# Split weights of a Strassen-Winograd mixture kernel: made in the tiles that TensorE reads, during the first of three chunks

## The chip, the cores and the metric

One core of a Trainium2 chip runs the whole program. The metric is the device time of one execution in microseconds (us). Engine names: PE is TensorE, DVE VectorE, ACT ScalarE, POOL GpSimd, SP SyncE, whose queue (SPq) issues nearly all DMAs.

## The reference, cut to what matters

```python
scores = (q @ k.T) / 8 + bias          # 4 batches, 8 heads, 768 rows, 64 wide; 8 global columns and 96 local ones are kept
x = softmax(scores) @ v                # laid out as 3072 rows x 512
p = domain_probs / (domain_probs.sum(-1, keepdims=True) + 1e-09)
out = 0
for e in range(4):                     # w1[e]: 512 x 1024, w2[e]: 1024 x 512
    h = max(x @ w1[e], 0)
    out += p[:, e:e+1] * (h @ w2[e])
```

## The kernel before, in words

**Stage A, attention.** `attention` (line 338) is a generator of 48 two-tile steps `d`, run by the loop at line 792. Each step turns scores into a 128x256 piece of x. The rows of x fall into three chunks of 1024. The pieces of chunk 0 stay in SBUF (the tiles `x0`, named b11 to b22, trace name `b`); those of chunks 1 and 2 go to DRAM (`xt` to `xd`). Beside the steps the loop runs other generators: `mixture` (288, the normalised p, from step 26), `spread_shares` (731, p transposed and stored in DRAM, from step 30), `first_forms` (672, from step 26) and `advance` (617), which prepares weights.

**Products.** All four matrices of a product are cut 2x2, and a Strassen-Winograd scheme with seven products takes the place of eight: the weight side needs A11, A12, A22 and the sums S1 to S4, the other side B11, B21, B22 and T1 to T4. Each operand is split in two parts, `hi` (a cast to fp32r) and `lo` (the rest, subtracted), and each product is hi·hi + lo·hi + hi·lo: six matmuls of 128x512 for one product of the first layer (`product`, 650, PSUM `pm`) and six for one half of a product of the second (`half`, 902, PSUM `pq`). The casts are on ACT, the subtractions on DVE or POOL.

**Chunks.** For each chunk there are 16 first-layer items `ci` (256 hidden units each) and 8 second-layer items `cj` (512 hidden units). The loop at line 982 counts slots `s`; 14 slots make a block `j` of two `ci`, and slot `r` of a block runs one first-layer product (`small`, 840, kk = 0 to 6) and one half product of the block before (`half`). So 24 blocks and a tail of halves. `form` (833) splits a sum of h into tiles `f1` to `f5` (trace name `f`). At kk = 6 of the second `ci`, T2 of h is written to the tile X (trace name `hX`) and T3 in place of B22 (`hB`); T2 is split at r = 1 of the next block on DVE, T3 at r = 3 with its `lo` on POOL, and T4 at r = 0, on DVE in chunk 0 and on POOL later. At kk = 4 of the next block, DVE writes the new B22. In the last block of a chunk `load_x`, `sum_x` and `next_form` (699 to 726) prepare x of the next chunk.

**Weights.** `prepare` (528) loads 256 rows or columns of w1 or w2 (`raw`), makes four sums on POOL, casts and subtracts in four groups into the tile `split` (pool `outp`, two buffers), and `store` (576) writes each group to DRAM (`kept`; trace names `w`, `w_A`, `w_S`). A `split` tile takes its buffer two groups after its predecessor, and the store of that predecessor is issued just before. There are 32 such preparations in 192 steps: 58 steps in stage A (line 788; there the casts are on POOL) and the rest in chunk 0 (`pace`, line 981; casts on ACT). TensorE never reads `split`: `ask_w1` (627) and `ask_w2` (639) load the parts back from DRAM into `w1s` (six buffers) and `w2s` (four buffers), in all three chunks.

**Order.** SP and POOL keep the program's order (`Kept`, line 48) all through, and so do the casts of weights. In stage A all engines do. In the chunks DVE, ACT and PE are ordered by the framework's scheduler, by dependencies and its own estimates.

Of the kernel before, what the change touches and what calls it, by code (L numbers as in the profile page):

```python
# [18 lines left out]
P = 128  # L19
# [181 lines left out]
def attn_moe_kernel(ctx: ExitStack, tc, q, k, v, n_global, n_local, domain_probs, w1, w2, out):  # L201
# [9 lines left out]
    W1BUFS = 6  # L211
# [314 lines left out]
    GROUPS = (("A11", "A12"), ("S1", "S2"), ("S3", "S4"), ("A22",))  # L526

    def prepare(kind, i, cast):

        e, g = divmod(i, NPR)  # L530
        raw = rawp.tile([P, 2, HALF], F32, name="raw")
        if kind == 1:
            flat = raw.rearrange("p n (a f) -> p (n a) f", f=2 * P)
            sy.dma_start(flat, w1[e, :, g * 2 * P : (g + 1) * 2 * P].rearrange("(a p) f -> p a f", p=P))
            four = raw.rearrange("p n (a m f) -> p n m a f", a=2, m=2)
            a11, a21, a12, a22 = (four[:, n, m] for n in range(2) for m in range(2))
            firsts = four[:, :, 0]
        else:
            sy.dma_start(raw, w2[e, g * 2 * P : (g + 1) * 2 * P, :].rearrange("(f p) m -> p f m", p=P))
            a11, a21, a12, a22 = (raw[:, n, m * 2 * P : (m + 1) * 2 * P] for n in range(2) for m in range(2))  # L540
            firsts = raw[:, :, : 2 * P]
        yield
        sums = rawp.tile([P, 2, HALF], F32, name="raw")
        quarters = [sums[:, n, m * 2 * P : (m + 1) * 2 * P] for n in range(2) for m in range(2)]
        if kind == 1:
            s1, s2, s3, s4 = (t.rearrange("p (a f) -> p a f", a=2) for t in quarters)
        else:
            s1, s2, s3, s4 = quarters
        po.tensor_add(s1, a21, a22)
        po.tensor_sub(s2, s1, a11)  # L550
        yield
        po.tensor_sub(s3, a11, a21)
        po.tensor_sub(s4, a12, s2)
        yield
        pairs = [t.rearrange("p (n c) -> p n c", n=2) for t in (sums[:, 0], sums[:, 1])]
        for n, names in enumerate(GROUPS):
            while len(stores) > 1:
                store()
            made = outp.tile([P, 2, 2, 2 * P], F32R, name="split")
            hi, lo = (made[:, : len(names), m] for m in range(2))  # L560
            if n == 0:
                src = firsts
            elif n == 3:
                hi, lo, src = hi[:, 0], lo[:, 0], a22
            else:
                src = pairs[n - 1]
            if kind == 1 and n in (0, 3):
                hi, lo = (t.rearrange("p n (a f) -> p n a f" if n == 0 else "p (a f) -> p a f", a=2) for t in (hi, lo))
            cast(hi, src)
            po.tensor_tensor(lo, src, f32(hi), op=ALU.subtract)  # L570
            stores.append((kind, i, n, made))
            yield

    stores = []

    def store():
        kind, i, n, made = stores.pop(0)
        if kind == 1:
            some = slice(0, len(GROUPS[n]))
            to = kept[(1, i, n)] = dp.tile([P, len(GROUPS[n]), 2, 2 * P], F32R, name=f"w1_{i}_{n}")  # L580
            sy.dma_start(f32(to), f32(made[:, some]))
            return
        j, u = divmod(i, 2)
        for at, name in enumerate(GROUPS[n]):
            if (2, j, name) not in kept:
                kept[(2, j, name)] = dp.tile([P, 2, 2, 2 * P], F32R, name=f"w2_{j}_{name}")
            sy.dma_start(f32(kept[(2, j, name)][:, u]), f32(made[:, at]))

    items = [(1, 0), (1, 1), (1, 2), (2, 0), (2, 1), (1, 3)]
    for i in range(2, per, 2):  # L590
        items += [(1, i + 2), (2, i), (2, i + 1), (1, i + 3)]
    items = [it for it in items if it[1] < per]
    going = {"now": None, "next": None, "done": 0.0, "cast": nc.gpsimd.tensor_copy}

    def cast(out, src):
        tc.keep_in_program_order(going["cast"](out, src))  # L596

    def step_weights():

        if going["now"] is None and items:  # L600
            going["now"] = prepare(*items.pop(0), cast)
            next(going["now"])
            going["at"] = 0
        if going["now"] is None:
            while stores:
                store()
            return False
        if going["at"] == 2 and items:
            going["next"] = prepare(*items.pop(0), cast)
            next(going["next"])  # L610
        next(going["now"], None)
        going["at"] += 1
        if going["at"] == 6:
            going["now"], going["next"], going["at"] = going["next"], None, 0
        return True

    def advance(steps):
        going["done"] += steps
        while going["done"] >= 1.0:
            going["done"] -= 1.0  # L620
            step_weights()
# [3 lines left out]
    ORDER2 = (("A11", "B11"), ("A12", "B21"), ("S1", "T1"), ("S2", "T2"), ("S4", "B22"), ("S3", "T3"), ("A22", "T4"))  # L625

    def ask_w1():
# [7 lines left out]
        sy.dma_start(f32(t[:, : len(names)]), f32(kept[(1, ci % per, n)]))  # L635
# [3 lines left out]
    def ask_w2():  # L639
# [7 lines left out]
        sy.dma_start(f32(t), f32(kept[(2, cj % NJ, name)]))  # L647
        w2t[(cj, name)] = t

# [22 lines left out]
    def first_forms(T1):  # L672

        b11, b12, b21, b22 = (x0[n] for n in BLOCKS)
        for k in range(2):
            def form(name, src):
                x_form(name, src, po, (k,), k == 0)
            form("B11", b11)
            po.tensor_sub(T1[:, k], b12[:, k], b11[:, k])
            yield  # L680
            form("B21", b21)
            yield
            form("T1", T1)
            po.tensor_sub(b12[:, k], b22[:, k], b12[:, k])
            yield
            form("T3", b12)
            po.tensor_add(b11[:, k], b12[:, k], b11[:, k])
            yield
            form("T2", b11)
            po.tensor_sub(b21[:, k], b21[:, k], b11[:, k])  # L690
            yield
            form("T4", b21)
            yield
            form("B22", b22)
            yield
# [3 lines left out]
    def load_x(c):  # L699
# [355 lines left out]
```

## Time and profile before

| | us |
|---|---|
| median of 2 runs | 1401.97 (1399.25 to 1404.68) |
| the profiled execution | 1399.54 |
| its span, first to last instruction | 1397.7 |
| PE busy (matmul) | 1198.4, 86% of the span |
| DVE / POOL / ACT busy | 852.4 / 567.9 / 493.7 |

The span is shorter than the time of the execution by what lies before the first and after the last instruction, 1.8 us. A line of the timeline has start, duration, engine, line, operation, out<-in, shape and count (instructions of one kind may be merged), and in brackets the idle time of the engine before it and what ended it. L42 and L57 are the wrappers through which all engines are called, so tiles tell the places.

### The profile page before, as it was taken

How to read it: one execution, taken by the hardware profiler on the slowest of the kernel's cores; microseconds unless marked ns; L12 is line 12 of the kernel's file. 1: busy time of each engine (PE TensorE's matmuls, PEld its weight loads, DVE VectorE, ACT ScalarE, POOL GpSimd, SP SyncE). 2: the span in 40 equal slices, each digit the busy share in tenths (PEclk: the TensorE clock that was granted, in tenths of full speed). 3: DMA queues.
4: the chain of work that ended last, by engine and by line, in shares of the span. 5: the costliest groups of instructions: out<-in, count | busy, mean ns of one | idle time of the engine just before them, and what ended most of it. 6: DMA issues, size and time to landing. Idle time of an engine off the chain costs nothing.

```text
span 1397.7 us, 17631 instructions
## 1 busy us (share of the span) xinstructions
PE 1198.4 (86%) x6177; PEld 940.9 (67%) x6177; DVE 852.4 (61%) x1416; ACT 493.7 (35%) x1010; POOL 567.9 (41%) x449
## 2 busy tenths in 40 slices
PE   9996896876776667778599999999889999999996
PEld 7885675654554555556478777787668877777774
DVE  6885673534453454537964677766776656776763
ACT  6775672423222232223324222222334322222222
POOL 4546864556554554665622222222532122222221
PEclk9998998999988788889899999999999999999999
DMA  9998897777776767587567565665648655565623
GB/s 216 247 260 226 236 289 241 258 247 252 258 255 226 248 226 260 208 301 274 183 199 229 182 189 159 201 203 182 224 125 257 205 174 179 183 185 175 196 91 108
DMA packets 218623, 299.14 MB, mean 214 GB/s; under 512 B 113984, under 2 KB 144800, under 8 KB 218528
## 3 DMA queue, kind: packets, MB, share of 16 engines
q1 hardware_dynamic: 216784, 297.55, 66.7%
q8 instruction: 51, 0.84, 0.2%
q10 hardware_dynamic: 1744, 0.39, 0.1%
q14 instruction: 44, 0.36, 0.1%
HBM read 228.64 MB, written 69.26 MB: 213 GB/s over the span
## 4 chain that ended last, share of the span: by engine, by line
PE 41%; DVE 18%; POOL 12%; DMA 12%; issue 10%; ACT 4%; SPq 2%; POOLq 0%; ACTq 0%; DVEq 0%
PE pm L42 18%; PE pq L42 17%; DVE hB L42 7%; DMA w_S<-split 5%; POOL split L57 5%; DVE f L42 4%; DMA w<-split 4%; POOL f L57 4%; PE ps L42 4%; DVE sumC L42 3%; ACT f L42 2%; SPq L57 2%; PE pt L42 2%; DVE hX L42 2%; DVE pm L42 1%
## 5 line engine op out<-in xcount | busy, mean ns | idle before, releaser
L42 PE MATMUL pq<-f,w2s 128*128 128x512 f32 x2016 | 554.1, 411 | 130.9 <-DVE sumC L42 38.8
L42 PEld LDWEIGHTS pq<-f,w2s 128*128 128x128 f32 x2016 | 387.7, 196 | 250.7 <-DVE sumC L42 57.8
L57 POOL TENSOR_TENSOR f<-hB,f 128x1024 fp32r<-128x1024 f32 x89 | 215.5, 2421 | 515.3 <-ACT f L42 515.3
L42 DVE TENSOR_TENSOR sumC<-pq,sumC 128x512 f32<-128x512 f32 (+1 forms) x209 | 198.0, 948 | 207.7 <-PE pq L42 207.3
L42 PE MATMUL pm<-xT,w1s 128*128 128x512 f32 x1152 | 304.1, 397 | 7.8 <-ACT u L42 7.5
L42 PE MATMUL pm<-xB,w1s 128*128 128x512 f32 x864 | 240.2, 410 | 29.9 <-DVE hB L42 29.9
L42 PEld LDWEIGHTS pm<-xT,w1s 128*128 128x128 f32 x1152 | 217.6, 191 | 60.5 <-ACT u L42 14.7
L42 ACT CAST f<-hB 128x1024 fp32r<-128x1024 f32 x144 | 150.8, 1050 | 298.2 <-DVE hB L42 227.6
L57 POOL TENSOR_TENSOR split<-raw,split 128x512 fp32r<-128x512 f32 (+1 forms) x128 | 156.6, 1228 | 185.4 <-ACT split L596 179.9
L42 PEld LDWEIGHTS pm<-xB,w1s 128*128 128x128 f32 x864 | 169.3, 198 | 74.3 <-DVE hB L42 38.4
L42 ACT COPY u<-pm 128x512 f32<-128x512 f32 x96 | 56.2, 585 | 187.3 <-PE pm L42 156.8
L57 POOL TENSOR_TENSOR raw<-raw 128x256 f32<-128x256 f32 (+1 forms) x130 | 107.2, 843 | 16.2 <-DMA raw<-in_moe_w_dram 13.5
L42 DVE TENSOR_TENSOR hB<-pm,u 128x512 f32<-128x512 f32 x48 | 33.2, 691 | 131.2 <-POOL f L57 92.0
L42 DVE SCALAR_TENSOR_TENSOR hB<-pm,share 128x512 f32<-128x512 f32 x144 | 98.9, 687 | 14.3 <-DMA share<-shares 10.0
L42 DVE TENSOR_TENSOR f<-hB,f 128x1024 fp32r<-128x1024 f32 x55 | 87.9, 1599 | 25.0 <-ACT f L42 25.0
L42 ACT ACTIVATE pb<-pb,nmax 128x256 f32<-128x256 f32 (+1 forms) x192 | 91.8, 482 | 9.9 <-DVE nmax L42 9.9
L42 ACT COPY p<-pm 128x512 f32<-128x512 f32 x48 | 28.2, 587 | 173.0 <-PE pm L42 166.1
L596 ACT CAST split<-raw 128x256 fp32r<-128x256 f32 (+1 forms) x89 | 49.1, 564 | 105.4 <-DMA w<-split 54.5
L42 DVE TENSOR_TENSOR hB<-hB,hB 128x1024 f32<-128x1024 f32 x48 | 63.1, 1314 | 30.8 <-POOL f L57 29.9
L42 DVE COPY pT<-pt 128x512 f32<-128x512 f32 (+1 forms) x96 | 59.2, 643 | 33.4 <-PE pt L42 28.9
L42 DVE CUSTOM_DVE_ANT_0 pb<-pm,nbias 128x256 f32<-128x256 f32 (+1 forms) x192 | 64.5, 391 | 2.0 <-PE pm L42 1.9
L42 PE MATMUL pm<-early_k,early_q 64*128 64x256 f32 (+1 forms) x384 | 52.8, 394 | 7.0 <-ACT early_k L42 6.7
(107 smaller groups left out, 958.9 us busy)
## 6 DMA issues: line engine op xcount, KB each, us to landing
w1s<-w SPq DMA_DIRECT2D x144, 512.0 KB, 4.7
w2s<-w_S SPq DMA_DIRECT2D x96, 512.0 KB, 4.4
w2s<-w_A SPq DMA_DIRECT2D x72, 512.0 KB, 4.0
w<-split SPq DMA_DIRECT2D x48, 512.0 KB, 3.7
raw<-in_moe_w_dram SPq DMA_DIRECT2D x32, 512.0 KB, 4.4
w_S<-split SPq DMA_DIRECT2D x64, 256.0 KB, 4.2
w_A<-split SPq DMA_DIRECT2D x48, 256.0 KB, 2.9
w1s<-w SPq DMA_DIRECT2D x48, 256.0 KB, 3.4
```

What stands on the lines that cost most here:

```text
L42: ins = fn(*args, **kwargs)
L57: return self.tc.keep_in_program_order(fn(*args, **kwargs))
L596: tc.keep_in_program_order(going["cast"](out, src))
```

## The change

What it does: (1) In stage A six w1 items and two w2 items (`EARLY`) are prepared, now a w2 item at a time (512 rows), in buffers of `w1p`, and each is stored when two or three later groups have been made. (2) The ten other w1 items and six other w2 items are made in chunk 0 by `ask_w1` and `ask_w2` themselves: the cast (ACT) and the subtraction (POOL) write the `w1s` or `w2s` tile that TensorE reads, and the tile is stored from there to DRAM for chunks 1 and 2 (`keep_fresh`). (3) The sums of weights are made in place in the raw tile. (4) The groups of w1 are cut otherwise, `w1s` has five buffers in place of six, and asks are issued one slot later in the program (`soon`/`due`). (5) T3 of h goes to X and T2 in place of B22. (6) `first_forms` makes sums a step or more before their cast and subtractions a step behind; `mixture` waits three steps more before DVE's reciprocal, and `spread_shares` starts at step 35. (7) x of the next chunk is loaded and split in another order (`border`). The pools `rawp` (3) and `outp` (2) become `raw1p` (2) and `raw2p` (4).

```diff
-    W1BUFS = 6
+    W1BUFS = 5
...
         po.tensor_scalar(total, total, 1e-9, None, op0=ALU.add)
         yield
+        yield
+        yield
+        yield
         tc.keep_in_program_order(ve.reciprocal(psumm, psumm))
...
-    GROUPS = (("A11", "A12"), ("S1", "S2"), ("S3", "S4"), ("A22",))
+    GROUPS = (("A11", "A12"), ("S1", "A22"), ("S2",), ("S3", "S4"))
+    EARLY = ((1, 0), (1, 1), (1, 2), (2, 0), (1, 5), (2, 7), (1, 9), (1, 13))
...
+    def make(kind, i, n, to, cast):
+        if kind == 1:
+            four = raws[(1, i)].rearrange("p n (a m f) -> p n m a f", a=2, m=2)
+            a11, a21, a12, a22 = (four[:, r, m] for r in range(2) for m in range(2))
+            if n == 1:
+                po.tensor_sub(a11, a11, a21)
+                po.tensor_add(a21, a21, a22)
+            elif n == 2:
+                po.tensor_sub(a21, a22, a11)
+            elif n == 3:
+                po.tensor_sub(a12, a12, a21)
...
+        cast(hi, src)
+        po.tensor_tensor(lo, src, f32(hi), op=ALU.subtract)
+    def keep(kind, i, n, made):
+        some = len(GROUPS[n]) if kind == 1 else 2
+        to = kept[(kind, i, n)] = dp.tile([P, some, 2, 2 * P], F32R, name=f"w{kind}_{i}_{n}")
+        sy.dma_start(f32(to), f32(made[:, :some]))
+    def prepare_early():
...
+            for n in range(4 if kind == 1 else 7):
+                if len(stores) > 2:
+                    keep(*stores.pop(0))
+                t = w1p.tile([P, 2, 2, 2 * P], F32R, name="w1s")
+                make(kind, i, n, t, po.tensor_copy)
+                stores.append((kind, i, n, t))
+                yield
...
     def ask_w1():
         t = w1p.tile([P, 2, 2, 2 * P], F32R, name="w1s")
-        sy.dma_start(f32(t[:, : len(names)]), f32(kept[(1, ci % per, n)]))
+        if ci >= per or (1, ci) in EARLY:
+            sy.dma_start(f32(t[:, : len(names)]), f32(kept[(1, ci % per, n)]))
+        else:
+            make(1, ci, n, t, ac.copy)
+            fresh[(1, ci, n)] = t
+            if n == 3:
+                load_late(1)
...
     def ask_w2():
...
+        else:
+            make(2, cj, n, t, ac.copy)
+            fresh[(2, cj, n)] = t
+            if n == 6:
+                load_late(2)
...
+    def keep_fresh(kind, i, n):
+        if (kind, i, n) in fresh:
+            keep(kind, i, n, fresh.pop((kind, i, n)))
...
+    def border(c, r):
+        if r == 2:
+            load("b11", "b12")
+        elif r == 5:
+            nextx["T1"] = raw1p.tile([P, 2, HALF], F32, name="raw1")
+            po.tensor_sub(nextx["T1"], nextx["b12"], nextx["b11"])
+        elif r == 7:
+            load("b21", "b22")
+            x_form("B11", nextx["b11"], po)
+        elif r == 9:
+            x_form("T1", nextx["T1"], ve)
...
-                b11, b12, b21, b22, t2 = (hb[n] for n in ("B11", "B12", "B21", "B22", "X"))
-                ve.tensor_sub(b22, b22, b12)
+                b11, b12, b21, b22, t3 = (hb[n] for n in ("B11", "B12", "B21", "B22", "X"))
+                ve.tensor_sub(t3, b22, b12)
                 ve.tensor_sub(b12, b12, b11)
                 form("T1", b12, ve)
-                ve.tensor_add(t2, b22, b11)
-                ve.tensor_sub(b21, b21, t2)
+                ve.tensor_add(b22, t3, b11)
+                ve.tensor_sub(b21, b21, b22)
...
             small(ci, kk)
-            if kk in (1, 3):
-                ask_w1()
-            if kk == 6:
-                ask_w1()
-                ask_w1()
-            if c == 0:
-                advance(pace * (0.5 if j == 0 else 1.0))
+            soon += [(ask_w1,)] * {1: 1, 5: 2, 6: 1}.get(kk, 0)
+            if kk in (0, 2, 3, 4):
+                soon.append((keep_fresh, 1, ci, (0, 2, 3, 4).index(kk)))
         if cj > 0:
             half(cj - 1, r // 2, r % 2)
+            if r % 2 == 0:
+                soon.append((keep_fresh, 2, cj - 1, r // 2))
+            else:
+                soon.append((ask_w2,))
             if r == 0:
                 form("T4", hb["B21"], ve if c == 0 else po)
             elif r == 1:
-                form("T2", hb["X"], ve)
+                form("T2", hb["B22"], ve)
             elif r == 3:
-                form("T3", hb["B22"], po)
+                form("T3", hb["X"], po)
+        for fn, *args in due:
+            fn(*args)
+        if c + 1 < CH and j == NJ - 1:
+            border(c + 1, r)
```

## Rows read from the trace of the kernel before

**Rows 1.** Busy time by stretch: span, PE, PEld, DVE, ACT, POOL, clock, DMA share, GB/s
```profile
279.00:690.00 411.00, 295.27 (x1087) 221.40 (x1088) 208.21 (x206) 116.18 (x171) 233.85 (x186) 0.86 0.70 246
731.00:985.00 254.00, 244.06 (x1061) 195.60 (x1059) 171.22 (x184) 74.24 (x91) 57.96 (x25) 1.00 0.62 196
```

**Rows 2.** Timeline of DVE: the sum written to X, once near each block's end
```profile
264.99 1.21 DVE L42 TENSOR_TENSOR hX<-hB,hB 128x1024 f32<-128x1024 f32 x1
...
637.80 2.32 DVE L42 TENSOR_TENSOR hX<-hB,hB 128x1024 f32<-128x1024 f32 x1
690.60 1.22 DVE L42 TENSOR_TENSOR hX<-hB,hB 128x1024 f32<-128x1024 f32 x1
...
979.67 1.22 DVE L42 TENSOR_TENSOR hX<-hB,hB 128x1024 f32<-128x1024 f32 x1
1032.04 1.22 DVE L42 TENSOR_TENSOR hX<-hB,hB 128x1024 f32<-128x1024 f32 x1
...
1361.90 1.22 DVE L42 TENSOR_TENSOR hX<-hB,hB 128x1024 f32<-128x1024 f32 x1
```

**Rows 3.** Waits, 279 to 690 us: who waited for whom, total us, times, longest
```profile
POOL split L57 <- ACT split L596: 155.4, 57, 7.1
...
DVE hB L42 <- POOL f L57: 66.6, 12, 11.1
...
ACT split L596 <- DMA w<-split: 39.5, 14, 6.2
...
PE pq L42 <- DMA w2s<-w_S: 28.1, 11, 8.8
```

**Rows 4.** Waits of SP's own queue in the same stretch
```profile
SPq L57 <- POOL split L57: 244.4, 59, 9.7
```

**Rows 5.** Timeline of stage A: the last piece of x of some steps, and one reciprocal
```profile
19.44 0.42 DVE L42 TENSOR_TENSOR b<-ps,rT 128x256 f32<-128x256 f32 x1
...
113.97 0.42 DVE L42 TENSOR_TENSOR xt<-ps,rT 128x256 f32<-128x256 f32 x1
...
128.86 0.30 DVE L42 RECIPROCAL psumm<-psumm 128x24 f32<-128x24 f32 x1 [12.54 <-POOL psumm L57]
...
130.75 0.42 DVE L42 TENSOR_TENSOR xt<-ps,rT 128x256 f32<-128x256 f32 x1
...
217.69 0.42 DVE L42 TENSOR_TENSOR xt<-ps,rT 128x256 f32<-128x256 f32 x1 [3.66 <-DMA b<-xt]
```

**Rows 6.** Timeline at the seam of stage A and chunk 0
```profile
226.57 0.32 SPq L57 DMA_DIRECT2D w<-split  x1
...
229.19 0.52 SPq L57 DMA_DIRECT2D share<-shares  x1
...
238.39 0.69 DVE L42 SCALAR_TENSOR_TENSOR hB<-pm,share 128x512 f32<-128x512 f32 x1 [10.04 <-DMA share<-shares]
```

**Rows 7.** Timeline at the start of a block of chunk 1
```profile
909.47 2.40 POOL L57 TENSOR_TENSOR f<-hB,f 128x1024 fp32r<-128x1024 f32 x1 [4.67 <-ACT f L42]
...
911.91 0.69 DVE L42 TENSOR_TENSOR hB<-pm,u 128x512 f32<-128x512 f32 x1 [2.99 <-POOL f L57]
...
912.65 1.23 PEld L42 LDWEIGHTS pm<-xB,w1s 128*128 128x128 f32 x6 [0.61 <-DVE hB L42]
```

**Rows 8.** Groups by shape, whole span: busy us, mean ns of one, idle before
```profile
L57 POOL TENSOR_TENSOR split<-raw,split 128x512 fp32r<-128x512 f32 x96 | 132.2, 1382 | 141.6 <-ACT split L596 139.1
...
L57 POOL TENSOR_TENSOR raw<-raw 128x256 f32<-128x256 f32 x128 | 102.1, 817 | 16.0 <-DMA raw<-in_moe_w_dram 13.5
...
L57 POOL TENSOR_TENSOR b<-b,b 128x512 f32<-128x512 f32 x6 | 7.7, 1276 | 0.0
```

**Rows 9.** Writers of and readers from X: ns min/median/max, first and last start
```profile
L42 DVE TENSOR_TENSOR f<-hX,f x24: 1208/2440/3042, 269.6 to 1365.9; 128x1024 fp32r<-128x1024 f32 x24
```

**Rows 10.** DMA issues: KB each, median us from issue to landing
```profile
w1s<-w SPq DMA_DIRECT2D x144, 512.0 KB, 4.7
...
w<-split SPq DMA_DIRECT2D x48, 512.0 KB, 3.7
```

More of the change, by code (lines that the diff above doesn't have):

```diff
@@ L524, in attn_moe_kernel @@
     x0, xb, kept = {}, {}, {}
[L526 to L531 removed]
+    GROUPS = (("A11", "A12"), ("S1", "A22"), ("S2",), ("S3", "S4"))
+    ORDER2 = (("A11", "B11"), ("A12", "B21"), ("S1", "T1"), ("S2", "T2"), ("S4", "B22"), ("S3", "T3"), ("A22", "T4"))
+    EARLY = ((1, 0), (1, 1), (1, 2), (2, 0), (1, 5), (2, 7), (1, 9), (1, 13))
+    raws = {}
@@ L542, in prepare @@
-        yield
[L543 to L571, printed above, removed]
-            yield
@@ L574, in attn_moe_kernel @@
[L574 to L621, printed above, removed]
+            raws[(1, i)] = raw
+            return
+        e, g = divmod(2 * i, NPR)
+        rows = w2[e, g * 2 * P : (g + 2) * 2 * P, :].rearrange("(u f p) m -> f p u m", u=2, p=P)
+        raws[(2, i)] = [raw2p.tile([P, 2, HALF], F32, name="raw2") for _ in range(2)]
+        for f in range(2):
+            sy.dma_start(raws[(2, i)][f], rows[f])
@@ L623, in attn_moe_kernel, with load_late @@
+    LATE = {
+        1: [(1, i) for i in range(per) if (1, i) not in EARLY],
+        2: [(2, j) for j in range(NJ) if (2, j) not in EARLY],
+    }
+    def load_late(kind):
+        if LATE[kind]:
+            load_raw(*LATE[kind].pop(0))
     w1t, w2t = {}, {}
     asked = {1: 0, 2: 0}
-    ORDER2 = (("A11", "B11"), ("A12", "B21"), ("S1", "T1"), ("S2", "T2"), ("S4", "B22"), ("S3", "T3"), ("A22", "T4"))
+    fresh = {}
     def ask_w1():
@@ new lines, in first_forms @@
+        src = {"B11": b11, "B21": b21, "B22": b22, "T1": T1, "T2": b11, "T3": b12, "T4": b21}
+        for name, add in (
+            ("B11", "T1"), ("B21", "T3"), ("T1", "T2"), ("T3", None), ("B22", "T4"), (None, None), ("T2", None), ("T4", None),
+        ):
+            for k in range(2):
+                while lows:
+                    lo, of, hi = lows.pop()
+                    po.tensor_tensor(lo, of, hi, op=ALU.subtract)
+                if add:
+                    sums(add, k)
+                if name:
+                    form(name, src[name], k)
+                yield
@@ new lines, in first_forms, with load @@
+        while lows:
+            lo, of, hi = lows.pop()
+            po.tensor_tensor(lo, of, hi, op=ALU.subtract)
+        yield
+    nextx = {}
+    def border(c, r):
+        def load(*names):
+            for n in names:
+                nextx[n] = raw2p.tile([P, 2, HALF], F32, name="raw2")
+                sy.dma_start(nextx[n], xd[(c, n)])
+        if r == 2:
[8 more added lines that the diff above has]
+            x_form("T1", nextx["T1"], ve)
+        elif r == 10:
+            x_form("B21", nextx["b21"], po)
+            ve.tensor_sub(nextx["b12"], nextx["b22"], nextx["b12"])
+        elif r == 11:
+            x_form("T3", nextx["b12"], po)
+            ve.tensor_add(nextx["b11"], nextx["b12"], nextx["b11"])
+        elif r == 12:
+            x_form("T2", nextx["b11"], ve)
+            ve.tensor_sub(nextx["b21"], nextx["b21"], nextx["b11"])
+        elif r == 13:
+            x_form("T4", nextx["b21"], ve)
+            x_form("B22", nextx["b22"], po)
@@ L805, in attn_moe_kernel @@
                 others.remove(o)
-        if d >= 4:
-            advance(DONE_IN_A / (STEPS - 3))
-        if d in (STEPS - 8, STEPS - 7, STEPS - 6, STEPS - 5, STEPS - 4, STEPS - 3)[: W1BUFS]:
+        if d >= 4 and early_w:
+            for _ in range(2 if d % 4 == 0 else 1):
+                next(early_w, None)
+        if d == STEPS - 5:
+            for _ in early_w:
+                pass
+            for kind in (1, 2, 1, 2):
+                load_late(kind)
+        if STEPS - 5 < d <= STEPS:
             ask_w1()
```

125 lines of the change are left out of this document (52 added, 73 removed).

## The prediction

> **What bounds the kernel now.** I read the busy time by stretch first, to see whether the three chunks cost the same; then the timeline of DVE, to get the length of single blocks; then the waits of the slow stretch, of the engines and of SP's queue; then stage A and its seam.
>
> A block ends near DVE's sum into X, so the distance between two such sums is one block's length. In chunk 0 the six blocks from 264.99 to 637.80 us take 372.8 us, 62.1 each; the eight of chunk 2 from 1032.04 to 1361.90 take 329.9, 41.2 each [rows 2]. Both have the same products; chunk 0 prepares weights beside them. The blocks in which the next x is made are alike, 52.8 us (637.80 to 690.60) and 52.4 (979.67 to 1032.04) [rows 2]. So about six times 21 us lie in chunk 0, and nearly none of that is TensorE's need: between 279 and 690 us PE is busy 295 of 411 us at a mean granted clock of 0.86, in chunk 1 244 of 254 at 1.00, the level of 2.4 GHz [rows 1].
>
> No engine is full in the slow stretch. POOL, the busiest helper, works 234 of 411 us [rows 1] and waits 155 us for ACT's casts of weights; those wait among others 39.5 us in 14 waits for stores of `w` from `split` to land; DVE waits 67 us for POOL's `f` parts, which stand behind the weights in POOL's order; PE waits 28 us for weights coming back [rows 3]. SP's queue waits 244 us for POOL's `split` before a store may go [rows 4], and behind such a store stand the loads of weights that PE needs. That is a ring: store, cast, subtraction, store, with two buffers, and PE's weights hang on it.
>
> Stage A starts regular: 25 steps from 19.44 to 113.97 us, 3.78 us each. At that pace the 46th step after the first would come at 193.3; it comes at 217.69, 24.4 us late [rows 5]. One gap alone, 113.97 to 130.75, loses 13.0 us: DVE stands at the reciprocal of the mixture for 12.54 us, and POOL, whose sum it wants, is behind in weights. At the seam the share of p is issued at 229.19, behind a store at 226.57, and DVE waits 10.04 us until 238.39 [rows 6].
>
> **The change, part by part.** The sum is made against the profiled execution, 1399.5 us (span 1397.7 and 1.8 around it), 2.5 us under the median of 1402.0.
>
> *Blocks of chunk 0.* Ten of 16 w1 items and six of 8 w2 items are now made in place; their loads back from DRAM go, the stores stay. What POOL must do in a block in which everything is fresh: two w1 items of four sums at 0.82 us, three subtractions at 1.38 and one of half size at about 0.7, 8.1 us each; one w2 item of four 512-wide sums at 1.28 and seven subtractions at 1.38, 14.8; three `f` parts at 2.40. Together 38 us [rows 7, 8]. Over chunk 0 it is 10 times 8.1, 6 times 14.8 and 8 times 7.2, 227 us: POOL fits a block of 41.2 us, barely in the full ones. The ring of stores is cut: a store reads a tile that was made some slots before, so SP need not wait for POOL at it, and PE's weights need no second trip. What is late next is ACT. A cast waits until PE has left the buffer and its store has landed, and behind it on ACT stand the copies p1, u2, u3 of the products (PE waits for u2 and u3 within a slot) and the casts of h; behind POOL's subtraction stand the `f` parts; SP waits for POOL only at the raw loads, after the last group of an item. The new length: 41.2, plus T4 on DVE in place of POOL (1.21 to 2.44 us for such an operation [rows 9], I take 1.8), plus DVE's other seven two-input operations of 1024, each some 0.4 longer when POOL is busy, half of them ahead of something PE waits for (1.4), plus casts in the way of copies, which no row shows: bounded by nothing (PE's own order hides it) and by the 155 us of POOL's waits over 6.6 blocks, 23 us each [rows 3]; I take 1.6, because the subtractions are due four slots or more after the ask. That is 46 us, 16 less than 62.1, and six blocks give 97. The lower end is 41.2 (125), the upper 56 (37): eight DVE operations at the longest of rows 9, 3.04 in place of 1.21 us.
>
> Here the Trainium skill speaks against the change. The trace has one and the same DVE operation at 1.21, 2.44 and 3.04 us [rows 9]. "SBUF — State Buffer", section "Who interferes with whom", says that a DVE instruction with two SBUF inputs contends with a GpSimd instruction that reads SBUF, and that the later one blocks until the first is done. By that, a POOL that is busy nine tenths of a block meets nearly every such DVE operation; it would put the block near the upper end, the time near 1331. I keep 46, since DVE's 1024-wide operations in chunk 0, with POOL busy 57% [rows 1], are not yet that slow.
>
> *Stage A.* Making and storing stay about as many (work of ten old items against 58 steps of six to an item). A buffer is now reused five groups later and its store goes two groups before that, so POOL seldom waits for a store; DVE's reciprocal comes three steps, 11 us, later than POOL's sum; casts of x no longer wait for a sum made in the same step. I take back the 13.0 and 4 of the other 11.4: 17 (8, if POOL stays as late; 24 at most) [rows 5].
>
> *The seam.* With no store waiting in SP's queue the share can go some 7 us earlier, after four loads of weights; but new raw loads (six of 512 KB) stand before it on the DMA engines. I take 6 of 10.0 (0 to 10) [rows 6]. In the first block, whose weights are all early, I take 4.
>
> *T2 and T3.* In chunks 1 and 2 DVE's new B22 waits 2.99 us for POOL's part of T3, whose source it overwrites; PE's weight load then waits 0.61 [rows 7]. With T3 in X this wait goes. T2's chain on DVE before it stays. I count 0.4 for 13 undisturbed blocks: 5 (0 to 8).
>
> *The rest.* One `w1s` buffer less and asks a slot later: the shortest lead, of S2, is still over four slots, 12 us, against a landing of 4.7 [rows 10]; nothing, with PE's next products as cover; if it were late, 1 us in each of 48 items. `border`: one more operation on DVE, loads split in pairs; 0, and 5 either way.
>
> Sum: 97 + 17 + 6 + 4 + 5 = 129; 1399.5 − 129 = **1270 us**.
>
> **The rivals.** *DVE and POOL in each other's way.* POOL's work comes denser, every sum and `lo` on DVE doubles, blocks take 56 us. For it: rows 9 and POOL's 38 us of work. Against: DVE has 171 of 254 us in chunk 1 [rows 1], so 14 us a block would just fit. 6 times 6.1 = 37, and with the other 32 the time is 1331.
>
> *Everything hidden.* Blocks of chunk 0 run as in chunk 2 less the T3 wait, 41 us, and stage A and seam lose nothing: 127 + 24 + 10 + 4 + 7 = 172, so 1228. For it: nothing is full. Against: a full block leaves POOL 3 us.
>
> *Stores in the way (slower).* The place: the cast into `w1s` or `w2s` must wait for the store of the group before in that buffer, and that store is issued in the slot just ahead of the ask. If SP is held at a raw load until POOL has finished, the store leaves late and each of some 15 casts of a block waits for a landing, 3.7 us [rows 10], with ACT's copies behind it and PE behind those. At half a landing, 1.85 us, the block is 46 + 28 = 74; six blocks cost 70 more than now, the rest still gives 32: 1438. It decides from 1.4 us per cast on (46 + 21 = 67.5, which eats the 32). Against it: a raw load waits for work due at the same time, not for a later store.
>
> *The ring moves, not the time.* Blocks stay at 62 because casts now wait for PE's release of the buffer as before for the store; half of stage A's gain and none of the seam: 1399.5 − 13 − 5 = 1382. Against: buffers are freed in PE's own order.
>
> **How the numbers follow.** Forecast 0.48; all hidden 0.20; DVE and POOL 0.20; no change 0.06; slower 0.06. A measurement of this kernel tells some 2% from no change, 1374 to 1430. The first three lie under that: 0.88, less a little for a crowded case that ends above 1374: 0.87 faster, 0.06 the same, 0.07 slower. The range runs from just under the all-hidden case, 1225, to past the crowded one, 1345, and leaves out under 2 in 10.
>
> **What would show it.** Right: sums into X 44 to 48 us apart in chunk 0, SP's wait for POOL gone from 244 us to a few tens, a granted clock over 0.93 there, no DVE wait of 12 us in stage A, no wait of `hB` for POOL's `f` in chunks 1 and 2, and block lengths there within 1 us. Wrong: ACT's casts waiting for stores or PE for over 3 us each; PE waiting for `w1s` or `w2s` made late; DVE's two-input operations at 3 us throughout; blocks of chunks 1 and 2 longer because a weight is not there.

## The result and the profile after

The changed kernel takes 1329.53 us (median of 2 runs, 1328.15 to 1330.9), 0.9483 of the kernel before, 95% interval 0.9394 to 0.9573. The gain is 72.4 us: the time lies in the stated range of 1225 to 1345, and the gain is little more than half of the 129 that the sum gave. The profiled execution's span is 1326.4 us, 71.3 less than before; the steps below are told against that.

First the timeline of DVE, the sums into X, as in [rows 2]:

```profile
244.06 1.21 DVE L42 TENSOR_TENSOR hX<-hB,hB 128x1024 f32<-128x1024 f32 x1
...
342.14 1.23 DVE L42 TENSOR_TENSOR hX<-hB,hB 128x1024 f32<-128x1024 f32 x1
402.76 1.23 DVE L42 TENSOR_TENSOR hX<-hB,hB 128x1024 f32<-128x1024 f32 x1
...
564.33 1.22 DVE L42 TENSOR_TENSOR hX<-hB,hB 128x1024 f32<-128x1024 f32 x1
629.23 1.21 DVE L42 TENSOR_TENSOR hX<-hB,hB 128x1024 f32<-128x1024 f32 x1
963.46 1.23 DVE L42 TENSOR_TENSOR hX<-hB,hB 128x1024 f32<-128x1024 f32 x1
1288.42 1.22 DVE L42 TENSOR_TENSOR hX<-hB,hB 128x1024 f32<-128x1024 f32 x1
```

The six blocks of chunk 0 take 320.3 us, 53.4 each. They are not alike: the third (342.14 to 402.76), in which two w1 items and a w2 item are made, takes 60.6, and the fifth 60.5; the others take 43 to 55. The block at the border takes 64.9. Chunk 2 takes 325.0, 40.6 a block. So the 71.3 us split up as follows.

| step | before, us | after, us | gain | predicted |
|---|---|---|---|---|
| 46th step of stage A | 217.69 | 209.41 | 8.3 | 17 |
| from there to the first sum into X | 47.3 | 34.7 | 12.6 | 10 |
| six blocks of chunk 0 | 372.8 | 320.3 | 52.5 | 97 |
| border block, chunk 0 to 1 | 52.8 | 64.9 | −12.1 | 0 |
| chunk 1 with its border | 341.4 | 334.2 | 7.2 | 5 with chunk 2 |
| chunk 2 | 329.9 | 325.0 | 4.9 | |
| tail | 35.8 | 38.0 | −2.2 | 0 |

Then the busy time of the six blocks, and of the third and fourth alone (columns as in [rows 1]):

```profile
244.00:564.00 320.00, 258.94 (x992) 202.04 (x992) 186.30 (x182) 103.87 (x151) 206.85 (x145) 0.89 0.47 167
...
342.00:403.00 61.00, 47.52 (x172) 36.96 (x171) 32.67 (x33) 18.37 (x29) 41.40 (x31) 0.83 0.46 164
403.00:452.00 49.00, 41.34 (x170) 32.77 (x169) 31.76 (x31) 16.41 (x24) 32.39 (x22) 0.93 0.52 182
```

POOL's 41.4 us of work in a full block lie near the 38 worked out, and a block of 60.6 us has 19 to spare. DVE has more room still, and the DMA engines are idle half the time. Again no engine is full; so the waits come next, from 287 to 564 us:

```profile
ACT w1s L42 <- POOL raw L57: 55.3, 21, 3.9
POOL w2s L57 <- ACT w2s L42: 42.5, 20, 5.6
ACT w2s L42 <- DMA w<-w2s: 40.3, 11, 6.6
POOL f L57 <- ACT f L42: 38.5, 14, 4.6
...
ACT w2s L42 <- POOL raw L57: 33.7, 10, 4.9
...
PE pm L42 <- ACT u L42: 19.3, 8, 3.8
PE pm L42 <- DMA w1s<-w: 18.1, 3, 6.6
...
PE pm L42 <- ACT p L42: 8.0, 5, 2.2
PE pq L42 <- ACT w2s L42: 7.2, 2, 4.4
```

ACT's casts of weights wait 89 us for POOL's sums (55.3 and 33.7) and 40 for stores. PE waits 27 us for ACT's copies `u` and `p`, 18 for loads of `w1s` and 7 for casts into `w2s`. The timeline of all engines shows how the first of these belongs to the casts, here 378 to 390 us:

```profile
378.97 1.61 SPq L57 DMA_DIRECT2D raw<-in_moe_w_dram  x3
380.62 0.47 SPq L57 DMA_DIRECT2D w<-w2s  x1
...
388.48 0.62 ACT L42 CAST w2s<-raw 128x512 fp32r<-128x512 f32 x1 [6.48 <-DMA w<-w2s]
389.01 0.58 ACT L42 COPY u<-pm 128x512 f32<-128x512 f32 x1
389.18 1.27 POOL L57 TENSOR_TENSOR w2s<-raw,w2s 128x512 fp32r<-128x512 f32 x1 [4.71 <-ACT w2s L42]
...
389.64 2.93 PE L42 MATMUL pm<-xT,w1s 128*128 128x512 f32 x6 [3.53 <-ACT u L42]
```

SP has stood 19.5 us for POOL before the raw loads. Then it issues them and seven stores of weights one after another; the first of these leaves at 380.62 and has landed at 388.40. The cast into its buffer stands until then; the copy `u` stands behind the cast, PE behind `u`, POOL behind the cast. At 364.92 to 366.07 us the same is seen with POOL's sum in the place of the store: a cast idle 2.59 us for `raw`, then `u`, then PE idle 3.33 us.

SP's queue, the row of [rows 4], from 279 to 690 us:

```profile
SPq L57 <- POOL w1s L57: 187.9, 11, 30.5
...
SPq L57 <- POOL w2s L57: 26.2, 11, 5.4
```

Its wait for POOL is 214 us after 244, in 22 waits for 59; it now stands at raw loads. "A few tens" was wrong.

Stage A, the rows of [rows 5] and the seam of [rows 6]:

```profile
125.97 0.42 DVE L42 TENSOR_TENSOR xt<-ps,rT 128x256 f32<-128x256 f32 x1 [2.75 <-DMA b<-xt]
...
130.78 0.27 DVE L42 RECIPROCAL psumm<-psumm 128x24 f32<-128x24 f32 x1
...
201.99 0.42 DVE L42 TENSOR_TENSOR xt<-ps,rT 128x256 f32<-128x256 f32 x1 [4.86 <-DMA b<-xt]
...
209.41 0.42 DVE L42 TENSOR_TENSOR xt<-ps,rT 128x256 f32<-128x256 f32 x1 [1.62 <-ACT rT L42]
...
217.79 0.50 SPq L57 DMA_DIRECT2D share<-shares  x1
...
226.41 0.69 DVE L42 SCALAR_TENSOR_TENSOR hB<-pm,share 128x512 f32<-128x512 f32 x1 [3.31 <-DMA share<-shares]
```

DVE no longer stands at the reciprocal (no bracket), yet pieces of x are late again, now because a buffer of `xt` has not been stored; at the seam 3.31 us are left of 10.04.

### The profile page after: what moved, and what is told of

It is laid out like the page before. It is cut to its first block, busy times and chain, and to the rows that moved or that the text cites. A ratio compares the mean times of both kernels' runs of the same rounds, so it can differ in the third digit from the quotient of the medians.

```text
span 1326.4 us, 17287 instructions
## 1 busy us (share of the span) xinstructions
PE 1185.4 (89%) x6177; PEld 946.0 (71%) x6177; DVE 871.1 (66%) x1418; ACT 490.8 (37%) x1003; POOL 571.0 (43%) x406
## 4 chain that ended last, share of the span: by engine, by line
PE 49%; DVE 20%; POOL 11%; issue 8%; DMA 7%; ACT 3%; SPq 1%; POOLq 0%; ACTq 0%; DVEq 0%
PE pm L42 21%; PE pq L42 19%; DVE hB L42 7%; PE ps L42 6%; POOL raw L57 5%; DVE f L42 5%; DVE sumC L42 3%; PE pt L42 3%; POOL w2s L57 2%; POOL w1s L57 2%; ACT f L42 2%; POOL f L57 2%; DMA w<-w2s 2%; DVE pm L42 1%; DVE hX L42 1%
## 5 line engine op out<-in xcount | busy, mean ns | idle before, releaser
L42 PE MATMUL pq<-f,w2s 128*128 128x512 f32 x2016 | 539.7, 402 | 56.5 <-DVE sumC L42 27.2
L42 PEld LDWEIGHTS pq<-f,w2s 128*128 128x128 f32 x2016 | 385.3, 193 | 161.0 <-DVE sumC L42 41.7
L57 POOL TENSOR_TENSOR f<-hB,f 128x1024 fp32r<-128x1024 f32 x65 | 158.9, 2445 | 510.8 <-ACT f L42 447.8
L42 PE MATMUL pm<-xT,w1s 128*128 128x512 f32 x1152 | 318.4, 413 | 39.5 <-ACT u L42 29.3
L42 PEld LDWEIGHTS pm<-xT,w1s 128*128 128x128 f32 x1152 | 226.8, 199 | 97.3 <-ACT u L42 36.9
L42 PE MATMUL pm<-xB,w1s 128*128 128x512 f32 x864 | 234.3, 398 | 22.9 <-DMA w1s<-w 18.1
L42 DVE TENSOR_TENSOR f<-hB,f 128x1024 fp32r<-128x1024 f32 x79 | 151.1, 1918 | 46.3 <-ACT f L42 46.3
L57 POOL TENSOR_TENSOR w1s<-raw,w1s 128x512 fp32r<-128x512 f32 (+1 forms) x78 | 95.2, 1222 | 26.6 <-ACT w1s L42 23.6
L57 POOL TENSOR_TENSOR f<-hX,f 128x1024 fp32r<-128x1024 f32 x24 | 57.6, 2399 | 96.7 <-ACT f L42 96.7
L57 POOL TENSOR_TENSOR raw<-raw 128x256 f32<-128x256 f32 (+1 forms) x72 | 78.2, 1087 | 2.0
L57 POOL TENSOR_TENSOR w2s<-raw,w2s 128x512 fp32r<-128x512 f32 x42 | 56.0, 1333 | 44.7 <-ACT w2s L42 44.7
```

The costliest lines, as they stand in the source:

```text
L42: ins = fn(*args, **kwargs)
L57: return self.tc.keep_in_program_order(fn(*args, **kwargs))
```

## Experiments

The first four kernels below ran beside one execution of the kernel before of 1405.69 us; four (casts on POOL, POOL's subtractions later, T2 and T3 as before, the share) beside one of 1404.31; three (T3's `lo`, the reciprocal, the early stores) beside one of 1404.74. Each time is one execution but for the last run. The changed kernel did not run again beside them, and those of the kernel before lie between 1395 and 1406 in this study, so differences of under 5 us are read from block lengths, not from times. Theory from here on: the blocks are held by the order in ACT's, POOL's and SP's queues, not by the work in them.

**Raw loads later.** The next raw load is issued four slots after the last group of an item, so that SP does not stand at it with stores behind.

```diff
             if n == 3:
-                load_late(1)
+                later.append((clock[0] + 4, 1))
...
+        while later and later[0][0] <= s:
+            load_late(later.pop(0)[1])
```

The three dots stand for the same edit at w2 items.

> The kernel after, with the raw loads of chunk 0 issued four slots later in SP's order; nothing else. Store theory: SP stands at each raw load until POOL has finished the item before (203 us of SP's waits in chunk 0), the stores behind it leave in a burst, ACT's casts wait for their landing (40 us) and the loads of early w1 items come late (18 us of PE). Then the six blocks, 53.4 us each in the kernel after, fall to 47 to 49 and the time by 25 to 40 us, to some 1295. Sum theory (ACT's casts wait for POOL's sums, 89 us): blocks stay at 51 or more, time above 1312. Port theory (DVE and POOL slow each other): no change, within 8 us of 1329.

1332.85 us, six blocks 323.5: no gain. SP's wait for POOL fell from 203 to 139 us between 244 and 564, and two rows are gone from the waits: the casts' for stores and PE's for loads of `w1s`. Others took their place (287 to 564 us):

```profile
POOL f L57 <- ACT f L42: 74.2, 15, 9.0
ACT w1s L42 <- POOL raw L57: 62.1, 21, 4.0
ACT w2s L42 <- POOL raw L57: 41.5, 15, 4.8
PE pm L42 <- ACT u L42: 18.9, 7, 3.1
```

PE's wait for `u` is the same 19 us; in the place of the 18 for loads it now waits for the sums of the second layer (`sumC`, DVE, 20.7) and for ACT's `f` (13.5).

**No stores of fresh weights.** `keep_fresh` issues nothing, and chunks 1 and 2 read the first items' weights in their place.

```diff
-            keep(kind, i, n, fresh.pop((kind, i, n)))
+            fresh.pop((kind, i, n))
+            kept[(kind, i, n)] = kept[(kind, 0, n)]
```

> The kernel after without the stores of fresh weights; in chunks 1 and 2 the parts of one early item are loaded in place of theirs, so that part of the computation is changed. It takes away the price of the stores altogether, with 38 MB of DMA. Store theory: at least as good as the later raw loads, blocks 46 to 49, time 1285 to 1305; what is left over 46 is sums and ports. Sum theory: blocks 51 or more. Port theory: no change.

1332.52 us, six blocks 323.7. Without any of those stores the six blocks take the same to 0.2 us as with the raw loads later. The 40 us of waiting for stores, read as a cost, cost nothing by themselves: the casts now wait 103 us for POOL's sums (62.1 and 41.3) in place of 89.

**Sums ahead.** POOL makes the sums for the next group right after its subtraction for this one, not just before the next cast.

```diff
-            if n == 1:
-                po.tensor_sub(a11, a11, a21)
...
         po.tensor_tensor(lo, src, f32(hi), op=ALU.subtract)
+        n = n + 1 if kind == 1 else n
+        if n == 1:
+            po.tensor_sub(a11, a11, a21)
+            po.tensor_add(a21, a21, a22)
+        elif n == 2:
+            po.tensor_sub(a21, a22, a11)
+        elif n == 3:
+            po.tensor_sub(a12, a12, a21)
```

> The kernel after, with POOL's sums for a group of weights emitted right behind the subtraction of the group before, so that ACT's cast finds them done; the work of POOL is the same. Sum theory: ACT's waits for POOL's sums (89 us in the 277 us of blocks 1 to 6) fall under 25, copies come in time, blocks 47 to 49, time some 1300. Store theory: the waits move to the stores, blocks 51 to 53, time above 1315. Port theory: within 8 us of 1329.

1317.34 us, six blocks 316.0, border 57.3: of the 12 us gained 4.2 lie in the blocks and 7.6 in the border. Between 287 and 564 us casts into `w2s` now wait 49.6 us for stores (14 times, up to 6.2) and 9.8 for sums: the other cover shows. Those into `w1s` still wait 61.9 us for sums, so that all waits for sums are 72 us and not under 25 as expected.

**Both together.**

> Raw loads four slots later and sums ahead together. If store and sum theory both hold and add up: blocks 44 to 47, the 46 of the prediction, time 1275 to 1290. If they are one wait seen twice: the same as the better of the two alone. Port theory: blocks stay over 51.

1297.88 us, six blocks 296.2, border 56.9. The loads alone gave nothing and the sums alone 12 us; together they give 32 of the changed kernel's 1329.5, and 24 of the six blocks' 320.3. Each wait had hidden the other. Between 287 and 537 us the casts still wait for POOL's sums, 106 us (84.0 and 22.5), yet PE's waits for `u` and `p` are down from 27 to 14 (9.6 and 4.7). POOL waits 55.7 us for ACT's cast of h, with the next sums queued behind it.

**Casts on POOL.** Raw loads later, and the casts of fresh weights on POOL in place of ACT.

```diff
-            make(1, ci, n, t, ac.copy)
+            make(1, ci, n, t, po.tensor_copy)
...
-            make(2, cj, n, t, ac.copy)
+            make(2, cj, n, t, po.tensor_copy)
```

> Raw loads four slots later, and the casts of fresh weights on POOL in place of ACT (some 0.6 us each, up to 9 us more for POOL in a full block, 47 in all); the sums stay where they are in the kernel after. Copy theory (what PE loses is the copies u2, u3 and p1 that stand in ACT's order behind a cast that waits for POOL): PE's waits for ACT's u and p (28 us over blocks 1 to 6) go, and blocks fall from 56 to under 52 although POOL has more to do; time some 1300 to 1315. POOL theory (POOL's work, with what it waits for, is the bound): full blocks get longer by about the 9 us, to 65 or more, time over 1340.

1313.92 us, six blocks 303.9. POOL works 267.4 us there (244 to 547) against 206.9 in the changed kernel, and the blocks are 16.4 us shorter in all, 19.6 shorter than with the raw loads later alone. Busy time of 60 us that hold its third block (339.09 to 389.50), and who waits (287 to 564, the last 16 us in the border block):

```profile
340.00:400.00 60.00, 48.50 (x188) 37.07 (x186) 40.91 (x37) 12.97 (x15) 57.90 (x48) 0.87 0.50 175
```

```profile
PE pm L42 <- POOL w1s L57: 34.7, 16, 6.3
PEld pq L42 <- POOL w2s L57: 19.5, 9, 4.9
POOL f L57 <- ACT f L42: 18.5, 6, 4.8
```

PE no longer stands at `u`; it waits for POOL, which is full, 57.9 of 60 us. The third block is 50.4 us long with 48.5 of POOL's work in it; the changed kernel's, 60.6 with 41.4, was therefore not held by the amount of POOL's work.

**POOL's subtractions of h later.** Both changes, and in chunk 0 POOL's `lo` of a sum of h is put two slots behind its cast, so that POOL goes on with weights meanwhile.

```diff
+        if low is po and clock[0] < NJ * 14:
+            lows.append((clock[0] + 2, t, src))
+        else:
             low.tensor_tensor(t[:, 1], src, f32(t[:, 0]), op=ALU.subtract)
...
+        due_lows(s)
```

`due_lows` issues, at the start of a slot, the subtractions that have come due.

> Raw loads later and sums ahead together, and besides in chunk 0 the subtractions of h on POOL stand two slots later in its order, where DVE and ACT have long made their source. Ring theory (POOL stands at the f parts until ACT's cast of h comes, 61 us over blocks 1 to 6, and the weights' sums stand behind them, for which ACT's casts wait, before PE's copies): POOL's wait for ACT's f falls under 20, blocks from 50.7 to 45 to 47, time from 1298 to about 1270. Port theory (POOL and DVE slow each other, POOL's work itself is the length): blocks stay at 50, time over 1290.

1282.14 us, 12 over the time expected, six blocks 278.6, 46.4 each, as expected, border 58.5. The busy times of its third and fourth block:

```profile
332.00:383.50 51.50, 45.50 (x183) 35.72 (x182) 32.29 (x32) 17.90 (x28) 41.92 (x31) 0.93 0.49 173
383.50:428.00 44.50, 38.18 (x155) 30.19 (x155) 31.28 (x32) 16.82 (x24) 32.58 (x22) 0.92 0.67 225
```

POOL's 41.92 us against 41.40 are the same work; the block is 9 us shorter. The waits (287 to 524) have no row of POOL's `f` any more, and the copies that held PE have shrunk:

```profile
ACT w1s L42 <- POOL raw L57: 62.6, 13, 7.3
...
PE pm L42 <- ACT u L42: 4.9, 2, 2.5
```

ACT still waits for sums, 63 us before `w1s` and 18 before `w2s`, 81 for the 89 of the changed kernel. What changed is that PE stands at `u` and `p` for 6 us, not 27. Of the 41.7 us by which the six blocks are shorter than the changed kernel's, 28 are idle time of PE, and 14 are PE's busy time, 259.2 us at a mean granted clock of 0.89 there and 245.4 at 0.93 here.

**T3's `lo` on DVE in chunk 0.** On top of that.

```diff
-                form("T3", hb["X"], po)
+                form("T3", hb["X"], ve if c == 0 else po)
```

> The kernel with raw loads later, sums ahead and POOL's subtraction of h two slots later, and besides T3's subtraction in chunk 0 on DVE, which takes 1.2 to 3.0 us a block from POOL and gives DVE about as much. Theory (in that kernel the full blocks, 51.5 us with POOL busy 42.0 of them, are bound by the order in which POOL and ACT hand the weights on, where POOL's length counts): full blocks 49 to 50.5, light ones 43.5 to 44.5, the time 5 to 10 us lower, 1272 to 1277 against 1282. Rival (TensorE, DVE and ACT in their own chain bound the block and POOL has slack): blocks the same or, with DVE's longer list, 0.5 to 1 us longer, and the time 1282 to 1288.

1275.2 us; six blocks 268.9, 9.7 less. The full ones, at 49.2 and 50.2, lose 2.4 and 1.1, as the theory had it; but the first, now 36.8, loses 3.4, and the other light ones, 43.3 to 45.0, lose 2.8 together. So once the order is right POOL's length counts, and not in the full blocks alone.

**T2 and T3 as before.** The changed kernel with that one part undone.

```diff
-                ve.tensor_sub(t3, b22, b12)
+                ve.tensor_sub(b22, b22, b12)
...
-                ve.tensor_add(b22, t3, b11)
-                ve.tensor_sub(b21, b21, b22)
+                ve.tensor_add(t2, b22, b11)
+                ve.tensor_sub(b21, b21, t2)
```

> The kernel after with T2 of h in X and T3 in place of B22, as before. Swap theory: blocks of chunks 1 and 2 go from 40.6 back to 41.3 us, 0.67 each, and the blocks of chunk 0, where POOL is late, lose more: DVE waits again for POOL's f before it writes hB (67 us in the kernel before); 3 to 8 us per block, time 1355 to 1385. Rival: POOL's part of T3 is not late any more in chunk 0, only the 0.67 in 16 blocks, time 1340.

1342.16 us, span 1340.4, 14.0 more than the changed kernel's. Plain blocks of chunks 1 and 2 take 41.3 again instead of 40.6; from the end of chunk 0's border to the last sum into X it is 668.5 us against 659.2, 9.3 more, and the tail is 2.4 shorter. The first block ends 3.0 later and chunk 0's six blocks take 4.0 more, little against the 52.5 that the change gained there. The 0.7 us a block is what [rows 7] had as PE's 0.61.

**The share before the raw loads.**

```diff
-            for kind in (1, 2, 1, 2):
-                load_late(kind)
...
     ask_share(0)
+    for kind in (1, 2, 1, 2):
+        load_late(kind)
```

> The kernel after with the six raw loads of the late items issued behind the share of p, not five steps before the end of stage A. DMA theory (the last steps of stage A wait for stores of xt, which stand behind 3 MB of raw loads: DVE 4.9 us at 201.99): the last step comes at some 205 in place of 209.4, and the first block ends 4 to 6 us earlier; time 1322 to 1326. Rival: nothing gained at the end of stage A, and block 1 waits for its raw data: time 1330 or more.

1331.74 us. The last pieces of x came 6 us sooner, the first block ended 3.6 us later (247.64), the second at 286.43 for 287.30: nothing in sum. The raw loads, 3 MB, now left behind the share, from 212.94 to 220.78 us, and the later data may have taken back what the earlier pieces gave; no run separates the two. The pieces are not without weight: with the early stores thinned, below, they come 9.2 us sooner and the second block ends 8.4 sooner, at 278.94.

**The reciprocal's place alone.** The kernel before with the reciprocal three steps later and the two following stage events moved as in the change.

```diff
         yield
+        yield
+        yield
+        yield
         tc.keep_in_program_order(ve.reciprocal(psumm, psumm))
...
-        if d == 30:
+        if d == 35:
             others.append(spread_shares())
...
```

> The kernel before, with its reciprocal and the two stage events behind it put off as in the changed kernel, and nothing else changed. Theory (the 12.5 us that DVE stood before the reciprocal were not the whole price of stage A, because the pieces that it held back afterwards met other waits): the 46th step, at 217.69 in the kernel before, comes at 208 to 213 and the time falls by 4 to 10 us, to about 1396 to 1401 where the kernel before takes 1405. Rival 1 (the reciprocal's wait is worth all it shows): the 46th step at 205 and the time 12 to 13 us lower. Rival 2 (the steps are bound by other work of DVE, ACT and TensorE anyway): the step stays at 215 to 218 and the time within 2 us of the kernel before.

1392.45 us, the 46th step at 214.71. DVE's pieces of x on its timeline:

```profile
118.10 0.42 DVE L42 TENSOR_TENSOR xt<-ps,rT 128x256 f32<-128x256 f32 x1 [0.41 <-ACT rT L42]
...
135.19 0.42 DVE L42 TENSOR_TENSOR xt<-ps,rT 128x256 f32<-128x256 f32 x1 [5.59 <-ACT rT L42]
...
214.71 0.42 DVE L42 TENSOR_TENSOR xt<-ps,rT 128x256 f32<-128x256 f32 x1 [3.62 <-DMA b<-xt]
```

The piece that came at 130.75 now comes at 118.10, 12.7 sooner; at the 46th step 3.0 are left. That is less than the theory's 5 to 10 (214.71 lies outside 208 to 213), and the span is 7.0 lower, 3.7 of it by the end of chunk 0. The time, 12.3 us under the one run beside it, fits rival 1, but the steps do not, and one run of the kernel before can be some us off; how much of the 12.3 is that stays open.

**Early stores thinned.** The changed kernel without the stores of early weights, but for the first item of each kind, which is read in place of the others.

```diff
-                    keep(*stores.pop(0))
+                    keep_first(*stores.pop(0))
...
```

> The changed kernel, with the stores of the early weights left out but for the first pair of each kind, whose kept weights are read in place of the others' (so the later pieces compute with other weights; loads, sums and casts of stage A stay as they are). Theory (in stage A the changed kernel's pieces wait for the stores of xt, because its weight stores fill the DMA queues: 13.0 us of DVE's waits between 105 and 225): those waits fall under 4 us, the 46th step comes at 197 to 202 instead of 209.41, and the time is 7 to 12 us lower than the changed kernel's (about 1321 to 1326 where that takes 1333). Rival (the pieces are late for DVE's and ACT's own work, and the stores' landing is only the last of several things that end together): the 46th step at 206 to 210, the time within 3 us.

1317.63 us, somewhat under the 1321 to 1326 expected. The 46th step comes at 200.20, 9.2 sooner, the first block ends at 234.49, 9.6 sooner. DVE's wait for stores of `xt` from 105 to 225 us, first the changed kernel, then this one:

```profile
DVE xt L42 <- DMA b<-xt: 13.0, 5, 4.9
```

```profile
DVE xt L42 <- DMA b<-xt: 4.4, 2, 3.4
```

The waits fall to 4.4 us, not under 4. The weights' stores did hold the pieces of x, and most of it in SP's queue: a piece is made, and its store leaves only when SP has issued what stands before it. In the changed kernel the piece of 146.24 is stored at 155.69:

```profile
146.24 0.42 DVE L42 TENSOR_TENSOR xt<-ps,rT 128x256 f32<-128x256 f32 x1 [0.83 <-ACT rT L42]
...
155.69 0.38 SPq L57 DMA_DIRECT2D b<-xt  x1
```

From the end of a piece to the issue of its store it is 7.0 us there (median of those made from 105 to 205 us; pieces and stores paired in their order), 2.7 before, and 2.0 with the stores thinned; SP is issuing DMAs for 87.8, 79.7 and 68.7 of the 105 us from 100 to 205. From issue to landing the medians of that stretch differ less, first the changed kernel, then this one:

```profile
b<-xt SPq DMA_DIRECT2D x24, 128.0 KB, 3.8
```

```profile
b<-xt SPq DMA_DIRECT2D x25, 128.0 KB, 3.0
```

The DMA engines carry 304 GB/s in the changed kernel, at a mean busy share of 1.03, 249 before (0.91), and 218 here (0.81).

**The best version in rounds.** T3's `lo` on DVE with the three changes of order, five times.

> The same kernel as the run before this one, timed in rounds: the changed kernel with raw loads later, sums ahead, POOL's subtractions of h two slots later and T3's on DVE in chunk 0. Theory (the waits that held the changed kernel's blocks above 46 us were those of the queues' order, and they are gone for good): 1270 to 1280 us, 0.904 to 0.914 of the kernel before. Rival (the single run was a lucky one, and part of the gain hangs on when transfers land): a median of 1283 to 1300, with runs that lie 5 us and more apart.

1269.34 us (median of 5, 1268.89 to 1273.78), 0.9069 of the kernel before, interval 0.9047 to 0.9090: 60 us under the changed kernel, 0.7 below the theory's range and far from the rival's. The sums into X of the profiled execution, the slowest of the five (1273.78):

```profile
247.33 1.21 DVE L42 TENSOR_TENSOR hX<-hB,hB 128x1024 f32<-128x1024 f32 x1
...
517.87 1.66 DVE L42 TENSOR_TENSOR hX<-hB,hB 128x1024 f32<-128x1024 f32 x1
574.00 1.21 DVE L42 TENSOR_TENSOR hX<-hB,hB 128x1024 f32<-128x1024 f32 x1
1233.30 1.22 DVE L42 TENSOR_TENSOR hX<-hB,hB 128x1024 f32<-128x1024 f32 x1
```

Six blocks take 270.5 us, 45.1 each, the border 56.1; from there to the last sum into X it is 659.3 us, as in the changed kernel (659.2). That this comes out at the predicted 1270 is chance in part: it is another kernel than the one predicted, and its blocks and the swap make up for stage A and the border.

## Why the prediction was right, and where it was wrong

The sign was right, and the traces bear out the reason: six blocks of chunk 0, where the fresh weights are made in TensorE's own tiles, fell by 52.5 us, most of the gain, and PE's 28 us of waiting for `w2s` to come back and DVE's 67 for POOL's `f` have no row there any more; for loads of `w1s`, of the early items, PE waits 18.1. That is read from the traces; no run has this part alone, and the swap of T2 and T3 accounts for 4.0 of the 52.5. The size was little more than half of the forecast's. That the time lies in the range is luck in part: the range reached past 1331 for DVE and POOL in each other's way, and that was not the cause. Of the signs for a right forecast, none of the six blocks took 44 to 48 us, the clock was 0.89 and not over 0.93, and SP's wait stayed; of those for a wrong one, casts into `w2s` waited for stores, 11 times and 3.7 us each.

*"Casts in the way of copies … I take 1.6."* This is the step that failed. The other terms of the block (41.2, 1.8 and 1.4) give 44.4; measured were 53.4, so the rest, put at 1.6, is 9.0 a block on the mean and 16 in a full one. This is a remainder, and not all of it is copies: over the six blocks PE waits 29.6 us for `u` and `p`, 4.9 a block, 18.1 for loads of `w1s`, 3.0 a block, and 7.2 for casts into `w2s`, 1.2 a block. The reason given, that subtractions are due four slots after the ask, looked at who needs the weight. It should have looked at who stands behind the cast. ACT works through its queue in order, as at 388.48 us above: a cast that waits for POOL's sum, or for a store, delays the copies of the products, and these PE needs within a slot. The runs show it: with sums ahead, raw loads later and POOL's `lo` of h out of the way, at the same work, PE's waits for `u` and `p` are 5.7 us over six blocks, those for loads of `w1s` are gone, and the block is 46.4 where 46 was predicted: the order was worth 7.0 us a block.

*The rival of the stores in the way* had the place right (SP held at a raw load, the store late, the cast behind it, 40 us of such waits), and its price was nothing alone: without the stores the blocks are as long. Once the sums are made ahead, putting the raw loads later is worth 19.8 us of the six blocks (316.0 to 296.2). In its sum 46 + 21 is 67, not 67.5; nothing hangs on it.

*The rival of DVE and POOL in each other's way* gives 1331, almost the measured time, and still was not the cause: `f` on DVE out of `hB` (1024 wide) has a median of 1.69 us in the changed kernel's six blocks, against 1.23 before, but 1.63 in the kernel with subtractions later, whose blocks are 7 us shorter, and 1.75 with the casts on POOL. The extra of about 0.5 us an operation, taken as 0.4, was about right. The longest of these, 3.30 us, was covered from end to end by operations of POOL. The Trainium skill ("SBUF — State Buffer", section "Who interferes with whom") has it that a DVE instruction with two SBUF inputs contends with a GpSimd instruction that reads SBUF, and this operation agrees; another that POOL covered as fully took 1.32 us, and as a price of the block the contention was small here.

*"Stage A … I take back the 13.0 and 4."* The wait at the reciprocal went, as predicted, but 8.3 were gained instead of 17. Two things were missed: taken alone that wait is worth 3.0 us by the 46th step, since other waits follow; and the stores of weights stand before those of `xt` in SP's queue, so that DVE waits 13.0 us for buffers of `xt`. With the early stores thinned the gain is 17.5, by a way that the sum did not have.

*"`border` … 0, and 5 either way."* It cost 12.1. Fresh w1 and w2 groups are still made in that block, up to 605 us, most of them ahead of x's own parts on POOL, which works 46 us there against 31 before. With the sums ahead it is 57.3, and 56.1 in the best version; the cause of the 3 to 5 us left against before stays open.

*Seam, T2 and T3.* 10 predicted for seam and first block, 12.6 measured; of the share's wait 6.7 of 10.0 went (6 taken). T2 and T3: 5 predicted, 12.1 gained in chunks 1 and 2, of which the swap accounts for 9.3 and gives 2.4 back in the tail; 0.4 a block was taken where 0.7 went. DVE's wait of `hB` for POOL's `f`, 17.9 us in chunk 1 before, has no row after.

*"SP's wait for POOL gone."* It stayed at 214 us. 64 us less of it, with the raw loads later, changed no block as long as POOL's sums were late too; with the sums ahead the same move took 3.3 us off each block. What a waiting queue costs is what stands behind it and has nothing else to wait for.

## What to carry to other kernels

When work is moved onto an engine's in-order queue, price it by what is queued behind it and by what that waits for, not by how early its result is wanted: here casts with four slots to spare cost 7 us a block by their place in the order, and changing the order alone, at the same work, took 47 us off the time. Where two waits end together, removing one shows little or nothing; try both at once before either is called harmless.

## What the runs showed of the hardware that was not expected

The granted clock was lower where PE waited more: 0.83 in the changed kernel's third block (60.6 us), 0.93 in the same block with POOL's subtractions later (51.5 us), both means between the levels of 1.2 and 2.4 GHz. The matmuls took longer at the lower one: PE was busy 259.2 us over the changed kernel's six blocks (0.89) and 245.4 over those with the subtractions later (0.93), with 993 and 990 records. So a wait taken away gave back more than its own length, 14 us beside 28 in those blocks.

In stage A one queue, SP's, issues nearly all DMAs, and each issue takes its time: from 100 to 205 us SP was issuing for 87.8 us in the changed kernel, and a 128 KB store of `xt` left at the median 7.0 us after its data was made and landed 3.8 us later. With most stores of weights left out these were 68.7, 2.0 and 3.0. So small stores were late more by their place in the queue than by the DMA engines, though those were at a mean busy share of 1.03 and 0.81 in the two.
